# Requesting the first quarter of an output weight later, and longer warm-up matmuls between transposes

## The chip, the cores and the metric

The kernel runs on one core of a Trainium2 chip. The metric is device time in microseconds of one execution; the time before is the median of three runs. The profile is one execution taken by the hardware profiler, with a span of 687.3 us from its first to its last instruction.

## The reference

A causal depthwise convolution with seven taps (softmaxed weights, one set for each of eight groups of channels) feeds a two-layer network with a swish activation whose slope is learned:

```python
w = exp(weight - max(weight)); w = w / (sum(w) + 1e-9)      # 8 heads x 7 taps
y[b, s, h, g] = sum_k w[h, k] * x_pad[b, s + k, h, g]        # x: 8 x 4096 x 192, 6 zeros in front
h = y @ w_in                                                 # 32768 x 192 times 192 x 2048
g = h * sigmoid(beta * h)
out = g @ w_out                                              # 2048 x 192, result float32
```

## The kernel before, in words

The eight sequences are handled in pairs: a chunk is 512 tokens of two sequences, one on the lower 64 partitions and one on the upper 64, with the 192 channels as three groups of 64. There are 32 chunks. For each chunk the steady loop (from line 551) goes over 16 units `fc` of 128 columns of w_in: `hidden` (line 421) makes six matmuls of 512 columns into a PSUM tile `ph`, and ScalarE turns it into `g` with one Silu activation whose scale is beta. `output` (line 511) puts matmuls of the second layer between the units: a `Job` adds up 16 units times two blocks of 128 tokens in a PSUM slot `pa` or `pb`, then VectorE reduces it and it is stored. In the first chunk (s = 0) these begin with unit 6 (four pairs) and unit 7 (five pairs) in slot a; the fifth pair of unit 7 is the first to use unit 4 of w_out.

Since Silu with scale beta computes silu(beta * h), w_out is divided by beta once: `scale_w_out(i)` (line 314) multiplies quarter i of `w_out_raw` (units 4i to 4i + 3) by `beta_r` and rounds it to bf16. Quarters 0 and 1 are scaled on GpSimd (lines 360 and 362), quarters 2 and 3 on VectorE inside the first chunk. GpSimd also requests the w_in casts (`load_w_in`, line 205: a DMA that converts to bf16, in two halves of 64 partitions). Units 0 and 1 of w_in come instead by a plain load (`w_in_raw`, line 169) and a ScalarE cast (line 346).

All plain loads are requested on SyncE (its queue is q1 in the profile; the casts are q0), in the order of the program. Line 270 makes GpSimd wait for the softmax weights before it requests the casts of units 2 to 11 (lines 271 to 273). Line 275 then writes one column of `w_out_raw` on GpSimd; the load of that part must wait for this write, so SyncE stops there until GpSimd has requested the casts. After it come the w_out quarters, the load of chunk 2, the last quarter of w_out and the load of chunk 3. GpSimd's own queue goes on with: scale quarter 0 (waits for its load), request the last quarter of w_in (units 12 to 15), scale quarter 1 (waits for its load). [...]

Chunk 0 takes a way of its own. Its tokens are cast to `x0b` on VectorE (line 264), transposed on TensorE block by block (`transposes`, line 227, for four blocks), copied to `xt0` by ScalarE and VectorE (line 305), and convolved by matmuls with diagonal matrices (`diag_tap`, line 288). `fill(n, cols)` (line 216) issues n matmuls of zeros, whose result is not used: they keep TensorE active while it has nothing else to do. Chunk 1's first channel group is convolved on TensorE too (`conv1`, line 394), its other two by VectorE taps (`tap`, line 323), which run in the first chunk.

Of the kernel before, what the change touches and what calls it, by code (L numbers as in the profile page):

```python
# [17 lines left out]
def kernel(  # L18
# [17 lines left out]
    nc = tc.nc  # L36
# [96 lines left out]
    NW = 4  # L133
    FW = F // NW
    NQ = NF // NW
# [6 lines left out]
    w_out_raw = setup.tile([128, NF, D], FP32)  # L142
# [3 lines left out]
    def load_w_out(i):  # L146
        fcs = slice(i * NQ, (i + 1) * NQ)
        nc.sync.dma_start(out=w_out_raw[:, fcs, :], in_=w_out_v[:, fcs, :])
# [7 lines left out]
    def load_x(dst, t0, i):  # L156
        t = t0 + i * 2 * BLK
        nc.sync.dma_start(
            out=dst[:, i].rearrange("q h b d -> q h (b d)"),
            in_=x_v[0, t : t + 2 * BLK, :, :].rearrange("(q b) h d -> q h (b d)", b=2),  # L160
        )
# [6 lines left out]
    for r in range(2):  # L168
        nc.sync.dma_start(out=w_in_raw[r * DG : (r + 1) * DG], in_=w_in_v[:, :, 0:F0])
    load_x(x1, TOK, 1)  # L170
    load_w_out(0)

    zeros = setup.tile([128, 128], BF16)
    nc.vector.memset(zeros, 0.0)
# [13 lines left out]
        fill=0.0,  # L188
# [8 lines left out]
        fill=0.0,  # L197
# [18 lines left out]
    def fill(n, cols=TOK):  # L216
        zc = zeros.unsqueeze(1).to_broadcast((128, cols // 128, 128))
        for _ in range(n):
            nc.tensor.matmul(pf[:, 0, 0:cols], zeros, zc, start=True, stop=True)  # L219
# [7 lines left out]
    def transposes(pt, xb, b):  # L227
        for c in range(NG):
            nc.tensor.transpose(  # L229
                pt[:, c, :], xb[:, b, c].rearrange("q h p -> q (h p)"), ident_b  # L230
            )

    def tokens(xt, b):
        t = HALO + (b // 2) * 2 * BLK
        return xt[:, :, t : t + 2 * BLK].rearrange("p c (q b) -> p c b q", b=2)[:, :, b % 2]
# [3 lines left out]
    pw = in_a()[:, 0, 0:K]  # L239
    nc.tensor.matmul(pw, sel.rearrange("i h p -> i (h p)"), w8, start=True, stop=True)  # L240
    fill(3)
    nmax = setup.tile([128, 1], FP32)
    total = setup.tile([128, 1], FP32)
    cw = consts.tile([128, K], FP32)
# [10 lines left out]
    def diags(k0, k1):  # L255
        nc.vector.tensor_tensor(
            diag[:, k0:k1],
            ident.unsqueeze(1).to_broadcast((128, k1 - k0, 128)),
            cw[:, k0:k1].unsqueeze(2).to_broadcast((128, k1 - k0, 128)),
            ALU.mult,  # L260
        )
# [10 lines left out]
    for i in range(1, NW - 1):  # L272
        load_w_in(i * FW, (i + 1) * FW)

    nc.gpsimd.memset(w_out_raw[:, NQ, 0:1], 0.0)
    for i in range(1, NW - 1):
        load_w_out(i)
    load(2)
    load_w_out(NW - 1)
# [22 lines left out]
    for b in range(NB):  # L302
        pt = pts[b % 3][:, b // 3, 0 : NG * BLK].rearrange("p (c q) -> p c q", c=NG)
        transposes(pt, x0b, b)
        (nc.vector.tensor_copy if b == 2 else nc.scalar.copy)(tokens(xt0, b), pt)  # L305
        if b % 2:
            fill(1, 384 if b > 1 else 128)
    diags(2, 4)
    diags(4, K)
    pb = pf[:, 1, 0:NF]  # L310
# [315 lines left out]
```

## Time and profile before

| what | value |
|---|---|
| median of three runs | 689.9 us (690.95, 689.9, 689.1) |
| span of the profiled run | 687.3 us |
| TensorE matmuls busy | 681.8 us, 99% |
| ScalarE busy | 578.0 us, 84% |
| VectorE busy | 523.3 us, 76% |
| GpSimd busy | 10.2 us, 1% |
| w_out loads | 4 of 384 KB, 11.2 us from request to landing |
| w_in casts | 6 of 192 KB (8.5 us) and 2 of 96 KB (7.5 us) |

A row of a timeline gives start, length, engine, line, operation, output and inputs, and in brackets the idle time of the engine before it with what ended it. PE is TensorE's matmul, PEld its weight load, DVE is VectorE, ACT ScalarE, POOL GpSimd, SP SyncE; a q after the name means its sequencer. A matmul's end is modelled, and consecutive ones overlap in their records, so their spacing is read from the starts. Line numbers are those of the kernel before.

### The profile page before, as it was taken

Reading aid. Unit: us, or ns where it says so; the run is one execution under the profiler, and the core shown is the slowest. Engines: PE = TensorE matmul, PEld = TensorE weight load, DVE = VectorE, ACT = ScalarE, POOL = GpSimd, SP = SyncE. Lnnn points to the kernel's source line nnn. Section 1 sums busy time; section 2 is a strip of 40 time slices with the busy share of each in tenths; the row PEclk is TensorE's granted clock in tenths of the full one; section 3 lists DMA queues with packets and bytes.
Section 4 is the critical chain, followed back from the end, with each engine's and each line's share of the span. In section 5 each row is a group of like instructions: output and inputs, shape, how many; then the busy total and the mean of one; then the engine's idle time right before and its main releaser. Section 6 shows DMA issues by size and latency. Waiting matters only on the chain.

```text
span 687.3 us, 24341 instructions
## 1 busy us (share of the span) xinstructions
PE 681.8 (99%) x11311; PEld 520.4 (76%) x11311; DVE 523.3 (76%) x466; ACT 578.0 (84%) x529; POOL 10.2 (1%) x21
## 2 busy tenths in 40 slices
PE   8999999999999999999999999999999999999998
PEld 4777777777777777777777777777777777777777
DVE  7889877779777788777797777887777977777712
ACT  7988888888888888888888888888888888888893
POOL 4100000000000000000000000000000000000000
PEclk9999999999999999999999999999999999999999
DMA  9734433244343344332344332344423443322111
GB/s 234 185 101 117 111 94 103 57 103 117 99 101 83 71 116 116 94 99 67 92 117 105 96 98 58 111 117 105 92 67 88 117 111 94 100 58 60 49 36 59
DMA packets 121861, 67.06 MB, mean 98 GB/s; under 512 B 53264, under 2 KB 121760, under 8 KB 121760
## 3 DMA queue, kind: packets, MB, share of 16 engines
q1 hardware_dynamic: 120048, 64.12, 35.4%
q0 software_dynamic: 1664, 1.38, 1.2%
q8 instruction: 88, 1.44, 0.9%
q14 instruction: 13, 0.11, 0.1%
q10 hardware_dynamic: 48, 0.01, 0.0%
HBM read 29.89 MB, written 25.17 MB: 80 GB/s over the span
## 4 chain that ended last, share of the span: by engine, by line
PE 99%; DVE 1%; ACT 0%; issue 0%
PE ph L429 48%; PE pa L465 25%; PE pb L465 24%; PE pb L290 1%; DVE xt L383 0%; PE ph L219 0%; PE ph L290 0%; DVE x0b L222 0%; PE pa L290 0%; PE pa L240 0%; ACT xt L305 0%; ACT cw L246 0%; PE pb L373 0%; PE pa L229 0%; PE pb L229 0%
## 5 line engine op out<-in xcount | busy, mean ns | idle before, releaser
L437 ACT ACTIVATE g<-ph,beta 128x1024 bf16<-128x1024 f32 x511 | 568.6, 1115 | 94.0 <-PE ph L429 89.7
L465 PEld LDWEIGHTS <-g 64*128 64x128 bf16 x8160 | 370.0, 94 | 103.0 <-issue 0.2
L429 PE MATMUL ph<-ct,w_in_s 64*128 64x512 bf16 x3066 | 423.3, 376 | 0.0
L328 DVE SCALAR_TENSOR_TENSOR ct<-xt,cw,ct 128x1536 bf16<-128x1536 bf16 (+2 forms) x189 | 337.2, 1784 | 2.5
L465 PE MATMUL pa<-w_out_s,g 64*128 64x192 bf16 x4112 | 244.0, 243 | 0.0
L465 PE MATMUL pb<-w_out_s,g 64*128 64x192 bf16 (+1 forms) x4048 | 230.0, 243 | 0.0
L429 PEld LDWEIGHTS <-w_in_s 64*128 64x128 bf16 x3072 | 159.3, 94 | 53.6 <-issue 0.7
L483 DVE TENSOR_REDUCE osb<-pa 128x384 f32<-128x768 f32 x64 | 61.3, 958 | 122.6 <-PE pa L465 121.7
L483 DVE TENSOR_REDUCE osb<-pb 128x384 f32<-128x768 f32 x63 | 60.3, 958 | 29.0 <-PE pb L465 29.0
L106 DVE CAST xb<-xf 128x768 bf16<-128x768 f32 x60 | 40.5, 677 | 0.0
L326 DVE TENSOR_SCALAR ct<-xt,cw 128x1536 bf16<-128x1536 bf16 (+1 forms) x31 | 30.8, 993 | 0.0
L481 ACT COPY osb<-pb 128x192 f32<-128x192 f32 x1 | 0.3, 319 | 7.2 <-PE pb L465 7.2
L207 POOL DMA_DIRECT2D w_in_s<-in_moe_w_in_dram x8 | 5.2, 656 | 0.0
L290 PE MATMUL pb<-xt,diag 64*128 64x512 f32 (+1 forms) x21 | 4.6, 435 | 0.3 <-DVE xt L383 0.3
L219 PE MATMUL ph<-zeros 128*128 128x512 bf16 (+2 forms) x9 | 3.7, 526 | 1.1 <-DVE warm L176 1.1
L121 DVE COPY xt<-xt 128x18 bf16<-128x18 bf16 x27 | 4.4, 162 | 0.0
L290 PEld LDWEIGHTS pb<-xt,diag 64*128 64x128 f32 (+1 forms) x21 | 2.8, 186 | 1.2 <-PE ph L429 0.8
L316 POOL TENSOR_TENSOR w_out_s<-w_out_raw,beta_r 128x768 bf16<-128x768 f32 x2 | 3.3, 1648 | 5.9 <-DMA w_out_raw<-in_moe_w_out_dram 5.9
L177 ACT ACT_TABLE_LOAD x1 | 1.3, 1283 | 1.8 <-PEq L610 1.8
L219 PEld LDWEIGHTS <-zeros 128*128 128x128 bf16 x9 | 0.9, 120 | 1.9 <-DVE warm L176 1.1
L229 PEld LDWEIGHTS <-x0b 128*128 128x128 bf16 x12 | 0.7, 97 | 1.7 <-DVE x0b L222 1.7
L316 DVE TENSOR_TENSOR w_out_s<-w_out_raw,beta_r 128x768 bf16<-128x768 f32 x2 | 1.9, 952 | 0.0
(59 smaller groups left out, 29.9 us busy)
## 6 DMA issues: line engine op xcount, KB each, us to landing
out_dram<-osb SPq DMA_DIRECT2D x127, 192.0 KB, 2.3
xf<-in_x_dram SPq DMA_DIRECT2D x60, 384.0 KB, 4.2
xt<-xb SPq DMA_TRANSPOSE x120, 2.9
x<-in_x_dram SPq DMA_DIRECT2D x4, 384.0 KB, 4.7
w_out_raw<-in_moe_w_out_dram SPq DMA_DIRECT2D x4, 384.0 KB, 11.2
w_in_s<-in_moe_w_in_dram POOLq DMA_DIRECT2D x6, 192.0 KB, 8.5
w_in_raw<-in_moe_w_in_dram SPq DMA_DIRECT2D x2, 192.0 KB, 6.8
w_in_s<-in_moe_w_in_dram POOLq DMA_DIRECT2D x2, 96.0 KB, 7.5
```

Source lines behind the costliest of these rows:

```text
L106: nc.vector.tensor_copy(xbs[ch][:, :, :, h, :], xfs[ch][:, h].rearrange("q b (p c) -> q b c p", c=NG),)
L121: nc.vector.tensor_copy(dst, last[:, :, HALO + TOK - PAD :])
L207: nc.gpsimd.dma_start(out=w_in_s[r * DG : (r + 1) * DG, :, c0:c1], in_=w_in_v[:, :, c0:c1])
L219: nc.tensor.matmul(pf[:, 0, 0:cols], zeros, zc, start=True, stop=True)
L290: nc.tensor.matmul(pv, diag[rows, k, :], xt[rows, o : o + TOK], start=(k == 0), stop=(k == k1 - 1),)
L316: (nc.vector if i > 1 else nc.gpsimd).tensor_tensor(w_out_s[:, fcs, :], w_out_raw[:, fcs, :], beta_r[:, fcs].unsqueeze(2).to_broadcast((12 ...
L326: nc.vector.tensor_scalar_mul(dst, src, scalar)
L328: nc.vector.scalar_tensor_tensor(out=dst, in0=src, scalar=scalar, in1=added, op0=ALU.mult, op1=ALU.add)
L429: nc.tensor.matmul(ph[:, h, :], w_in_s[rows, j, fc * 128 : (fc + 1) * 128], cts[s][rows, j, :], start=(j == 0), stop=(j == last),)
L437: nc.scalar.activation(gs[s][:, fc], ph, AF.Silu, scale=beta[:, fc : fc + 1])
L465: nc.tensor.matmul(self.po[:, r, b * D : (b + 1) * D], g[rows, fc, self.h, q * BLK : (q + 1) * BLK], w_out_s[rows, fc, :], start=(self.don ...
L483: nc.vector.tensor_reduce(dst, self.po[:, :, 0 : nb * D].rearrange("p r n -> p n r"), axis=mybir.AxisListType.X, op=ALU.add,)
```

## The change

The first quarter of w_out is no longer requested early, ahead of the w_in casts. All quarters now stand behind the one-column write on GpSimd, which is moved to quarter 0: the casts of units 2 to 11 get the DMA engines first. Beside it the zero matmuls around chunk 0's transposes are made longer by 128 columns each in three places (after the three fills that follow the softmax matmul, after block 1 and after block 3), so that TensorE's pauses there are shorter.

```diff
@@ -168,7 +168,6 @@
     for r in range(2):
         nc.sync.dma_start(out=w_in_raw[r * DG : (r + 1) * DG], in_=w_in_v[:, :, 0:F0])
     load_x(x1, TOK, 1)
-    load_w_out(0)
 
@@ -239,6 +238,7 @@
     nc.tensor.matmul(pw, sel.rearrange("i h p -> i (h p)"), w8, start=True, stop=True)
     fill(3)
+    fill(1, 128)
     nmax = setup.tile([128, 1], FP32)
@@ -272,8 +272,8 @@
     for i in range(1, NW - 1):
         load_w_in(i * FW, (i + 1) * FW)
 
-    nc.gpsimd.memset(w_out_raw[:, NQ, 0:1], 0.0)
-    for i in range(1, NW - 1):
+    nc.gpsimd.memset(w_out_raw[:, 0, 0:1], 0.0)
+    for i in range(NW - 1):
         load_w_out(i)
     load(2)
     load_w_out(NW - 1)
@@ -304,7 +304,7 @@
         (nc.vector.tensor_copy if b == 2 else nc.scalar.copy)(tokens(xt0, b), pt)
         if b % 2:
-            fill(1, 384 if b > 1 else 128)
+            fill(1, 512 if b > 1 else 256)
     diags(2, 4)
```

## The prediction

> **What bounds the kernel now.** I read the busy shares first, then stages of the first 20 us, the chain, the timeline of GpSimd and VectorE, and the DMA queues. The busy shares and the busiest rows:
>
> ```profile
> PE 681.8 (99%) x11311; PEld 520.4 (76%) x11311; DVE 523.3 (76%) x466; ACT 578.0 (84%) x529; POOL 10.2 (1%) x21
> ```
>
> TensorE is busy 681.8 of 687.3 us. The stages say where the other 5.5 us lie (columns: stretch, its length, busy time and count of PE, PEld, DVE, ACT, POOL, granted clock, DMA share, GB/s):
>
> ```profile
> 0.00:4.34 4.34, 3.28 (x9) 1.21 (x9) 0.81 (x7) 2.10 (x5) 1.41 (x9) 1.00 0.51 151
> 4.34:7.14 2.80, 2.03 (x18) 0.92 (x16) 2.69 (x9) 2.55 (x6) 2.55 (x5) 1.00 0.99 281
> 7.14:11.30 4.16, 4.16 (x19) 3.15 (x20) 3.44 (x7) 2.64 (x5) 1.71 (x4) 1.00 1.14 274
> 14.50:14.83 0.33, 0.00 (x2) 0.04 (x2) 0.29 (x2) 0.33 (x2) 0.33 (x1) 1.00 1.19 239
> 14.83:20.00 5.17, 5.17 (x55) 3.57 (x57) 5.06 (x4) 4.92 (x6) 2.11 (x2) 1.00 1.15 276
> ```
>
> Idle are 1.06 us at the start, 0.77 us between 4.34 and 7.14, 0.33 us at 14.5, the rest in the tail after the last matmul. From 14.83 on TensorE never rests: whatever delays it there is added to the end, and nothing later gives it back. In the pauses before 7.14 it is not the bound; the chain there runs over other engines:
>
> ```profile
> 4.53 0.64 DVE x0b L222 x2
> 5.17 0.33 DVE diag L256
> 5.50 0.34 DVE x0b L222
> 5.83 0.05 issue
> 5.88 0.34 PE pa L229 x3
> 6.22 0.34 PE pb L229 x3
> 6.56 0.02 issue
> 6.58 0.51 ACT xt L305
> 7.10 0.04 issue
> 7.14 0.96 PE pa L290 x3
> ```
>
> The moved transfer feeds GpSimd, whose whole queue after 4.8 us is this (start, length, instruction, idle time before it):
>
> ```profile
> 4.83 3.91 POOL L207 DMA_DIRECT2D w_in_s<-in_moe_w_in_dram  x6
> 8.73 0.12 POOL L275 MEMSET w_out_raw<- 128x1 f32 x1
> 12.40 1.47 POOL L316 TENSOR_TENSOR w_out_s<-w_out_raw,beta_r 128x768 bf16<-128x768 f32 x1 [3.55 <-DMA w_out_raw<-in_moe_w_out_dram]
> 13.82 1.29 POOL L207 DMA_DIRECT2D w_in_s<-in_moe_w_in_dram  x2
> 17.47 1.83 POOL L316 TENSOR_TENSOR w_out_s<-w_out_raw,beta_r 128x768 bf16<-128x768 f32 x1 [2.37 <-DMA w_out_raw<-in_moe_w_out_dram]
> ```
>
> So it waits for the first quarter of w_out until 12.40, scales it, requests the last quarter of w_in, then waits for the second quarter until 17.47.
>
> [...] (2) [...] while GpSimd scaled at 17.47 to 19.30, the VectorE tap begun at 18.01 took 2.37 us where its neighbours take 1.285, and GpSimd finished 1.32 us after the tap before had ended (17.98). (3) [...] In this trace full clock is recorded from 4.34 us, 3.28 us after the first matmul, and held: the favourable case.
>
> **The short matmuls.** They add 128 columns after the three fills, 128 after block 1 and 128 after block 3. A cold 512-column fill spaces 0.426 us from the next (1.461, 1.887, 2.314), so 128 columns are 0.107 us cold[...]. The first falls into the 0.23 us in which TensorE waits for x0b (4.66 to 4.90), the second into the 0.26 us before 5.88, the third with the 0.23 us transpose of beta into the 0.27 us before 7.14. VectorE's casts and ScalarE's copy hide all three: **cost 0**. Their gain is 0 in a run whose clock is full at 4.34. [...] the cold stretch could run into the 17 diagonal matmuls after 7.14, spaced 0.23 us warm and at most 0.43 cold: 8 of them are 1.6 us. The three times before spread over 1.85 us, so this may be in them; for the median I take -0.1 us, bounds 0 and -1.6.
>
> **The moved request: what it removes.** Only one wait on w_in is visible: unit 4's first pair of matmuls starts at 15.36 and 15.54, where other pairs start within 0.04 us; its cast (second half) landed at 15.49, the trace says. Earlier casts give back **0.15 us**. Units 8 to 11 landed at 18.65 for a use at 20.08, so nothing is won there.
>
> **What it adds: a later landing.** The request goes from 4.34 to 8.88, when the memset releases SyncE; each of the other requests behind it shifts by its issue time, 0.4 us. Bounds from the trace: 12.4 (now; also 8.88 plus the 3.5 us of the first x load) and 17.34 (what the second quarter took, which was requested at this very 8.88). Between them I work with rates. Now w_out's bytes move in 8.7 to 10, then the casts almost alone, then both:
>
> ```profile
> q0 software_dynamic: 546, 0.39, 127.9%
> q1 hardware_dynamic: 25, 0.02, 3.8%
> ```
>
> ```profile
> q0 software_dynamic: 490, 0.47, 78.8%
> q1 hardware_dynamic: 451, 0.35, 38.6%
> ```
>
> The first pair is 10.5 to 12.5, the second 12.5 to 16: casts alone 0.195 MB/us; shared 0.134 and 0.100; q1 alone runs at 0.32 (0.58 MB in 16.2 to 18). The six casts are 0.98 MB, a quarter of w_out 0.39. If the casts take over at 8.7 and q1 joins at 12.5 as it did, casts have moved 0.74 by then and need 1.8 us more; q1 moves 0.18 in these and the rest in 0.66 us: 15.0, with some 0.5 us to completion (an estimate: almost nothing of the quarter moved after 11.5, and GpSimd was released at 12.4) **15.5**. If q1 joins at 10.0 (1.1 us after the request; the first request, at 0.81, shows its first bytes in the slice from 1 to 2 us), it needs 3.9 us: 14.4. If the casts do not start sooner than now, 17.3. I take 15.5.
>
> **Who is queued behind it.** GpSimd in order: scaling 0, the two requests for w_in's last quarter (1.29 us), scaling 1. At 15.5 VectorE is in a tap (taps stand back to back: one at 15.37 for 1.285, the next at 16.69). By (2) GpSimd starts at 16.66, ends at 17.98; first use of this quarter is at 18.68, in time. The requests take it to 19.3; scaling 1 meets the tap of 19.1 to 20.37 and ends at **21.7** instead of 19.30. Unit 7's last pair needs it at 19.98 (the tenth of the pa matmuls that start at 19.65): TensorE stands **1.7 us**. [...] The w_in requests come 4.2 us later, at 18.0 and 18.65; they took 7.5 and 8.4 us to land, 7.2 at best, so the second half lands at 25.9 to 27.1. Unit 12 uses it at 24.32, shifted to 26.0: 0 to 1.1 us more, which I take at 0 as the two overlap. VectorE loses nothing in sum: one collision with a tap before, one after, the other lying beside the PSUM evacuation of 20.3.
>
> **Sum:** 689.9 + 1.7 - 0.15 - 0.1 = 691.3.
>
> **The rivals.** A, the transfer is hidden anyway: w_out lands by about 13.5, scaling 0 runs beside copies out of PSUM, the second quarter's landing still decides scaling 1. For it: total bytes ahead of the second quarter are the same. Against: q1's gap of 10.5 to 12.5. 689.9 - 0.15 - 0.1 = 689.6. B, the landing is 17.3: GpSimd starts at 17.98, first use waits 0.6 us, requests at 19.3 and 19.95, scaling 1 done at 22.1 (2.1 us late), w_in's second half at 27.2 to 28.4 for 24.32: 2.8 to 4.0 us, say 693.2. For it: that is what the second quarter did from the same request time. C, the clock: the pauses now cost cold stretches in most runs and the fills end them: 688.4. Against: the profiled run (689.15 us) is warm at 4.34 already, and only 0.75 us under the median.
>
> **How the numbers follow.** Forecast 0.40 (spread 0.8 to 2.0 us over before), A 0.30, B 0.22, C 0.08. The bound of 0.3% is 2.07 us: slower are B and a tenth of the forecast's spread and a little more, 0.29; faster is half of C, 0.04; same 0.67. The range from 689.0 to 693.2 leaves out most of C and the late half of B.
>
> **What would show it.** Right: scaling 0 on GpSimd at 15 to 17.5 with its idle time ended by the w_out DMA, a TensorE pause of 1 to 2 us before the pa matmuls of unit 7, scaling 1 ending after 21. Step by step: x1b, taps and diagonal matmuls at the same times; unit 4's two halves within 0.04 us. A scaling that still starts before 13.5 makes A right; a pause at unit 12 for w_in makes B right; matmuls at 0.43 us spacing after 7.14 in the old trace only, or a median under 688.5, make C right. I would be wrong above all if the arbitration between the queues is not what the old order of bytes suggests.

## The result

The changed kernel takes **692.3 us** (median of six runs, 691.89 to 692.89) against 689.96 us before (six runs, 689.1 to 691.62): 2.3 us more, ratio 1.0031 with a 95% interval of 1.0018 to 1.0044. The forecast was 691.3, in a range that ends at 693.2. The direction, the place and the range were right. The loss was put too low (1.4 us forecast, 2.3 measured), and the two parts of the change do not add up as the forecast's sum supposed (experiments 1 and 2).

The profiled execution after the change spans 691.1 us. Its 3.8 us over the profile before are more than the medians' 2.3, because it is the longest of its six runs and the one before was among the shortest of its own; of what the runs before vary by, more below.

TensorE's busy time, first line of the page, rose by 1.4 us (683.2 for 681.8), so most of the 3.8 us is idle time:

```profile
PE 683.2 (99%) x11312; PEld 521.1 (75%) x11312; DVE 523.4 (76%) x466; ACT 578.0 (84%) x529; POOL 10.5 (2%) x21
```

It lies after 14.83 us, where TensorE never rested before. Stages, columns as before:

```profile
14.83:20.00 5.17, 4.79 (x44) 2.82 (x46) 5.06 (x4) 4.92 (x5) 2.89 (x3) 1.00 1.11 326
20.00:25.00 5.00, 3.75 (x57) 2.55 (x55) 4.95 (x6) 3.23 (x4) 1.91 (x2) 1.00 1.14 290
25.00:30.00 5.00, 3.75 (x56) 2.45 (x53) 3.49 (x7) 3.24 (x4) 0.00 (x0) 1.00 0.38 71
30.00:40.00 10.00, 10.00 (x166) 8.38 (x163) 5.83 (x7) 8.81 (x10) 0.00 (x0) 1.00 0.49 136
```

From 30 us on it is full again. TensorE's timeline names the stands, the stretches in which it waits. Two rows of the trace before, of the output matmuls of units 6 and 7 (the ninth matmul of the second row, which begins the fifth pair, starts at 19.98):

```profile
18.68 0.53 PE L465 MATMUL pa<-w_out_s,g 64*128 64x192 bf16 x8
19.65 0.61 PE L465 MATMUL pa<-w_out_s,g 64*128 64x192 bf16 x10
```

After the change (two stretches):

```profile
19.25 0.51 PE L465 MATMUL pa<-w_out_s,g 64*128 64x192 bf16 x8 [0.36 <-POOL w_out_s L316]
...
21.98 0.26 PE L465 MATMUL pa<-w_out_s,g 64*128 64x192 bf16 x2 [1.25 <-POOL w_out_s L316]
```

```profile
26.64 0.39 PE L429 MATMUL ph<-ct,w_in_s 64*128 64x512 bf16 x1 [0.16 <-DMA w_in_s<-in_moe_w_in_dram]
28.12 0.82 PE L429 MATMUL ph<-ct,w_in_s 64*128 64x512 bf16 x5 [1.10 <-DMA w_in_s<-in_moe_w_in_dram]
```

Scaling 0 is late for the first pa matmuls, scaling 1 for the fifth pair of unit 7, and the two halves of w_in's last cast are late for unit 12. Read by starts, the delay over the trace before grows from 0.57 us (19.25 for 18.68) to 2.0 (21.98 for 19.98) and to 3.6 and 3.8 (the two halves of unit 13, at 28.98 and 29.19 for 25.38 and 25.40). GpSimd's queue shows where all of it comes from:

```profile
17.11 2.09 POOL L316 TENSOR_TENSOR w_out_s<-w_out_raw,beta_r 128x768 bf16<-128x768 f32 x1 [8.24 <-DMA w_out_raw<-in_moe_w_out_dram]
19.15 1.29 POOL L206 DMA_DIRECT2D w_in_s<-in_moe_w_in_dram  x2
20.46 1.47 POOL L316 TENSOR_TENSOR w_out_s<-w_out_raw,beta_r 128x768 bf16<-128x768 f32 x1
```

GpSimd stands 8.24 us for w_out's first quarter, where it stood 3.55; the requests for w_in, which stand behind scaling 0 in its queue, go out at 19.15 instead of 13.82. The chain that ended last now has no work of TensorE between 3.5 and 28.1 us (its later part):

```profile
8.90 8.04 DMA w_out_raw<-in_moe_w_out_dram
...
17.11 2.09 POOL w_out_s L316
19.20 0.62 POOLq L621
19.82 8.26 DMA w_in_s<-in_moe_w_in_dram
...
28.12 0.69 PE ph L429 x5
```

Two transfers of 8 us, one requested only when the other has landed and been scaled.

### The profile page after: what moved, and what is told of

Its sections match the earlier page's. It is cut to its first block, busy times and chain, and to the rows that moved or that the text cites. A ratio compares the mean times of both kernels' runs of the same rounds, so it can differ in the third digit from the quotient of the medians.

```text
span 691.1 us, 24342 instructions
## 1 busy us (share of the span) xinstructions
PE 683.2 (99%) x11312; PEld 521.1 (75%) x11312; DVE 523.4 (76%) x466; ACT 578.0 (84%) x529; POOL 10.5 (2%) x21
## 4 chain that ended last, share of the span: by engine, by line
PE 96%; DMA 2%; POOL 1%; DVE 0%; ACT 0%; POOLq 0%; issue 0%
PE ph L429 47%; PE pa L465 24%; PE pb L465 24%; DMA w_in_s<-in_moe_w_in_dram 1%; DMA w_out_raw<-in_moe_w_out_dram 1%; POOL w_in_s L206 1%; POOL w_out_s L316 0%; PE ph L218 0%; POOLq L621 0%; PE pa L239 0%; ACT cw L246 0%; ACT osb L481 0%; POOL hold L270 0%; DVE cw L249 0%; DVE nmax L245 0%
```

## The experiments

The kernels of experiments 1 to 4 share one set of 30 runs of the kernel before (median 690.42 us), those of 5 to 8 another of 43 (690.24), those of 9 and 10 a third of 33 (689.62).

### 1 and 2: each part alone

```diff
 # 1, on the kernel before: the zero matmuls only
+    fill(1, 128)
-            fill(1, 384 if b > 1 else 128)
+            fill(1, 512 if b > 1 else 256)
 # 2, on the kernel before: the w_out request only
-    load_w_out(0)
-    nc.gpsimd.memset(w_out_raw[:, NQ, 0:1], 0.0)
-    for i in range(1, NW - 1):
+    nc.gpsimd.memset(w_out_raw[:, 0, 0:1], 0.0)
+    for i in range(NW - 1):
```

> The kernel before with only the longer zero matmuls. Theory 1 (the whole loss comes from the later w_out load, the zero matmuls cost nothing and save little): 689.3 to 690.0 us, ratio to before 0.999 to 1.000. Rival (the zero matmuls themselves delay the transposes): 690.5 us or more. Rival (the clock: they end a cold stretch that most runs of before have): 688.5 to 689.2 us with a narrower spread than before's 2.5 us.

> The kernel before with only the moved w_out request. Theory 1: 692.2 to 693.0 us, 2.3 to 3.1 above before; in its trace the scaling of quarter 0 on GpSimd starts near 17, TensorE stands three times: about 0.4 us before the first pa matmuls, 1.3 us before the fifth pair of unit 7, 1.3 us before unit 12. Rival (the zero matmuls are part of the loss): 691.5 us or less.

Measured: the zero matmuls alone 689.38 us (13 runs, ratio 0.9993, 0.9984 to 1.0001); the moved request alone 692.2 us (9 runs, ratio 1.003, 1.0019 to 1.0041), which are two groups, five runs at 691.7 to 692.2 and four at 693.1 to 693.2. So the loss is the request's: 1.8 us beside the 690.42 of the same set. Between kernel 1 and the changed kernel (692.3), which differ in it alone but were run in different sets, lie 2.9 us. The zero matmuls cost nothing. The interval does not show that they gain; the distribution points to it, with small counts: of the 30 runs before 13 were above 690.6 us, of kernel 1 one in 13. Once the request is moved no gain shows: 692.2 us without the longer zero matmuls, 692.3 with them.

The trace of kernel 2 fell into the upper group (693.13 us). Its TensorE after the transposes:

```profile
7.30 1.65 PE L289 MATMUL pa<-xt,diag 128*128 128x512 f32 x3
8.75 1.43 PE L289 MATMUL ph<-xt,diag 128*128 128x512 f32 x4
```

Three diagonal matmuls take 1.65 us where the profile before has 0.96; single ones start 0.427 us apart. In the clock's record full rate begins at 9.48 us here, at 4.34 in the profile before and at 5.55 in the changed kernel's. Yet the late clock does not make this run long. TensorE comes to the first pa matmuls 1.1 us late (19.82 for 18.68), and so does not wait for scaling 0 and stands only 0.45 us for scaling 1. Then it waits for w_in's second half, which lands at 28.29 (28.07 in the changed kernel), and unit 13's second half starts at 29.40, 0.2 us after the changed kernel's. The wait swallowed the cold stretch, and of the three stands expected there were two. Why kernel 2's runs fall into two groups stays open: no trace of the lower one was kept.

The start of full clock differs from trace to trace: in the 12 traces of this study it lies between 4.34 and 11.92 us. What decides on it is not shown.

### 3 and 5: what is queued behind the waiting scaling

```diff
 # 3, on the changed kernel: w_in's last quarter ahead of scaling 0
+    nc.gpsimd.tensor_copy(hold, beta_r[0:1, 0:1])
+    load_w_in((NW - 1) * FW, F)
     scale_w_out(0)
-    load_w_in((NW - 1) * FW, F)
     scale_w_out(1)
 # 5, on the changed kernel: w_in's last quarter behind scaling 1
     scale_w_out(0)
-    load_w_in((NW - 1) * FW, F)
     scale_w_out(1)
+    load_w_in((NW - 1) * FW, F)
```

> The changed kernel, with the requests for w_in's last quarter put ahead of the scaling of quarter 0 on GpSimd, behind a one-element copy that waits for beta_r (about 12.2 us). Theory 1a (what is queued behind the waiting scaling makes the larger part): the requests go out at 12.3 to 13.7, the stand at unit 12 (1.3 us) is gone, scaling 1 follows scaling 0 at once and ends near 20.6 instead of 21.9, so that the stand before it shrinks from 1.25 to some 0.3 us: 690.0 to 690.8 us. Rival 1b (the late landing alone makes the loss, the more so as the casts now also compete with w_out from 16 us on): w_out lands at 17.5 or later and the time stays at 691.7 or more.

> The changed kernel, with the scaling of quarter 1 put ahead of the requests for w_in's last quarter on GpSimd. Theory 3a (the last wait, for the second half of w_in's last quarter at unit 12, alone sets the loss and swallows the stands before it): the requests go out 1.5 us later than in the changed kernel, at 20.6 and 21.3, the second half lands near 29.5, and the time rises to 693.0 to 694.0 us although the stand before unit 7's fifth pair shrinks from 1.25 to below 0.4 us. Rival 3b (the stands for w_out make the loss): 691.0 to 691.6 us.

Measured: kernel 3 690.05 us (13 runs, 689.82 to 690.93), kernel 5 694.47 us (6 runs; ratio 1.0053, 1.0036 to 1.007). Both go the way of the queue: beside the changed kernel's 692.3 us, from another set, by 2.3 us down and 2.2 us up; counted from the kernel before in each one's own set, by 2.7 down and 1.9 up. In kernel 3, w_out lands hardly sooner (GpSimd is released at 16.37), yet most of the loss is gone. In kernel 5 the stand for scaling 1 has shrunk to some 0.3 us (the fifth pair of unit 7 starts at 20.33 for 20.00 undelayed, inside the first row of TensorE's), and still it is the slowest of all, a little above its expected range. Its GpSimd, and its TensorE:

```profile
16.23 4.05 POOL L316 TENSOR_TENSOR w_out_s<-w_out_raw,beta_r 128x768 bf16<-128x768 f32 x2 [7.37 <-DMA w_out_raw<-in_moe_w_out_dram]
```

```profile
19.67 0.91 PE L465 MATMUL pa<-w_out_s,g 64*128 64x192 bf16 x10
...
22.71 0.42 PE L465 MATMUL pb<-w_out_s,g 64*128 64x192 bf16 x6 [0.25 <-DVE ct L407]
27.41 0.39 PE L429 MATMUL ph<-ct,w_in_s 64*128 64x512 bf16 x1 [2.15 <-DMA w_in_s<-in_moe_w_in_dram]
28.42 0.82 PE L429 MATMUL ph<-ct,w_in_s 64*128 64x512 bf16 x5 [0.62 <-DMA w_in_s<-in_moe_w_in_dram]
```

The expected 29.5 for the second half was wrong: requested 1.07 us later than in the changed kernel (20.89 for 19.82), it landed only 0.3 us later, at 28.37. So the last wait is 0.3 us longer (28.42 for 28.12). The rest is clock, which no theory had: from 29.16 to 32.57 us the clock's record shows half rate (the mean granted clock is 0.92 from 25 to 30 us and 0.87 from 30 to 40; 1.00 in both in the changed kernel), by estimate half of these 3.41 us, 1.7 us, lost. The sum of 2.0 us is what lies between the two profiled runs (694.86 and 692.89). One of the six runs took 691.87 us; whether half clock was absent in it is not known, as it has no trace. Around the start of the half rate TensorE was less busy (from 25 to 30 us its matmuls filled 2.22 us, 3.75 in the changed kernel); that this is the cause is not shown. Without the clock kernel 5 stands about where the changed kernel does, though before unit 12 it was only 0.8 us late (unit 11 at 24.02 for 23.25), where that was 2.0: the wait for w_in's last quarter sets the loss, and swallows the stands for w_out before it. Kernel 3, which takes this wait away, confirms it from the other side.

When a load counts as complete varies by itself: five traces start alike (changed, 2, 3, 5 and 7), with the quarter's bytes moved at 15.1 to 15.2 us in each, and GpSimd is released at 17.11, 17.30, 16.37, 16.23 and 16.60. So the different releases of two of them say nothing about their edits.

### 4 and 6: when w_out is requested

```diff
 # 4, on the changed kernel: gate after four casts
     load_w_in(F0, FW)
-    for i in range(1, NW - 1):
-        load_w_in(i * FW, (i + 1) * FW)
+    load_w_in(FW, 2 * FW)
     nc.gpsimd.memset(w_out_raw[:, 0, 0:1], 0.0)
+    load_w_in(2 * FW, 3 * FW)
 # 6, on the changed kernel: gate after two casts
     load_w_in(F0, FW)
+    nc.gpsimd.memset(w_out_raw[:, 0, 0:1], 0.0)
     for i in range(1, NW - 1):
         load_w_in(i * FW, (i + 1) * FW)
-    nc.gpsimd.memset(w_out_raw[:, 0, 0:1], 0.0)
```

> The changed kernel, with the column write on GpSimd put ahead of the casts of units 8 to 11, so that w_out is requested at about 7.6 instead of 8.9 us. Theory 2a (a plain load requested while casts are on their way has its first bytes a fixed 3.6 us later): first w_out bytes at 11.2, quarter 0 lands near 15.7, 690.5 to 691.5 us. Theory 2b [...]: w_out quarter 0 flows directly behind x1 from about 8.7, lands near 12.5, and the time is that of before, 689.3 to 690.0 us. Theory 2c (only the amount of cast bytes ahead counts): first bytes near 11.8, landing near 16.3, 691.3 us or more.

> The changed kernel, with the column write on GpSimd put ahead of the casts of units 4 to 11, behind those of units 2 and 3 alone; w_out is requested at about 6.3 us. Theory 2a (first bytes a fixed 3.5 us after the request once casts are on their way): first w_out bytes at 9.8, mixed with casts; quarter 0 lands at 14.5 to 16, time 690.0 to 691.5. Theory 2b [...]: w_out behind x1 from 8.7, landing near 12.5 to 13.5, time 689.2 to 689.8, as with the early request and the zero matmuls.

Measured: kernel 4 692.63 us (5 runs), kernel 6 689.67 us (22 runs, ratio 0.9994, 0.9986 to 1.0001). In the packets' record w_out's first bytes flow at 11.3 us in kernel 4 and at 9.15 in kernel 6, 3.6 and 2.7 us after SyncE's request; behind the request of 8.9 us, before and after the change, it was 3.6 to 3.7. So the first bytes follow the request, as theory 2a has it, though the delay is not fixed: it was shorter with fewer casts ahead. That the casts are its cause is not shown: the kernel before requests quarter 0 at 4.34 us, ahead of every cast, and its first bytes flow at 8.40, behind the earlier loads of the same queue. And theory 2a's times failed in both kernels: kernel 4 lies in the range of 2c, whose landing stays near 17, kernel 6 in that of 2b. In kernel 4 the earlier bytes bought nothing. The two queues from 11 to 15 us there, and GpSimd:

```profile
q0 software_dynamic: 478, 0.45, 74.8%
q1 hardware_dynamic: 516, 0.39, 36.7%
```

```profile
17.09 2.27 POOL L315 TENSOR_TENSOR w_out_s<-w_out_raw,beta_r 128x768 bf16<-128x768 f32 x1 [8.29 <-DMA w_out_raw<-in_moe_w_out_dram]
```

By 15.0 q1 has moved 0.39 MB, as much as the quarter has, and still GpSimd is released two microseconds later. The changed kernel is alike: its packets reach that sum at about 15.15, its GpSimd starts at 17.11. Its queues from 15 to 16.5 us show what is left:

```profile
q1 hardware_dynamic: 601, 0.45, 103.0%
q0 software_dynamic: 23, 0.02, 7.8%
```

The casts still hold 7.8% of the engines' time, in a trickle. The traces keep 16 completion marks for each transfer. In kernel 2 the quarter has 15 of them by 16.00 us and the last at 17.12; in the changed kernel 13 by 15.98 and the last at 16.94; in kernel 5, released first, all 16 by 16.05. The last marks of w_in's last half straggle in the same way: 15 by 26.61 us and the last at 28.37 in kernel 5. That a few late marks of 16, at times a single one, end these waits is thus shown; what makes them late is not.

In kernel 6 w_out starts before the larger casts and is there in time:

```profile
13.14 1.47 POOL L316 TENSOR_TENSOR w_out_s<-w_out_raw,beta_r 128x768 bf16<-128x768 f32 x1 [4.34 <-DMA w_out_raw<-in_moe_w_out_dram]
```

### 7: the rest of kernel 3

```diff
 # on kernel 3
-    QUOTA_A = {6: 4, 7: 5}
+    QUOTA_A = {6: 4, 7: 4}
```

> The kernel with w_in's last quarter requested ahead of the scaling, and unit 7 of the first chunk given four pairs instead of five, so that quarter 1 is first used in unit 8, near 20.7 instead of 20.0 us. If the 0.4 us in which TensorE still stands between 20 and 25 us there is the wait for the scaling of quarter 1: 689.4 to 689.7 us, level with the zero matmuls alone (689.38). If it is the late end of the scaling of quarter 0 or another wait: 690.0 us, no change.

Measured: 690.05 us (14 runs), no change: what is left is set by another wait. Besides the 0.32 us before the fifth pair (20.32 for 20.00), which is gone in kernel 7, TensorE's timeline in kernel 3 has one stand between 16 and 30 us:

```profile
22.70 0.42 PE L466 MATMUL pb<-w_out_s,g 64*128 64x192 bf16 x6 [0.26 <-DVE ct L408]
```

Slot b waits for VectorE's evacuation of the diagonal convolution, which stands behind taps, and GpSimd's two scalings lie beside taps there (3.89 us for both, twice the 1.47 of each in kernel 6 are 2.94). The taps take longer too: the three beside the scalings 6.10 us in kernels 3 and 7, 5.01 in the kernel before, where one scaling lies beside them. In kernel 7 the stand for slot b is still there, 0.48 us long.

### 8, 9 and 10: the clock

```diff
 # 8, on the kernel before
-        if b % 2:
-            fill(1, 384 if b > 1 else 128)
 # 9 on kernel 6, 10 on kernel 1
-        if b % 2:
-            fill(1, 512 if b > 1 else 256)
+        if b != 2:
+            fill(1, (128, 384, 0, 512)[b])
```

> The kernel before without the two zero matmuls after blocks 1 and 3. Clock theory [...]: the runs fall apart into about 689.2 and 691.0 or more, more of them high than before (15 of 30 above 690.6 there), median 690.9 to 691.6. Rival (the pauses do not matter, the 1.0 us between before and the longer zero matmuls has another cause): 690.4 us and the same spread.

> The kernel whose column write on GpSimd stands behind the casts of units 2 and 3 alone (w_out requested at 6.3 us), with zero matmuls of 128, 384 and 512 columns after blocks 0, 1 and 3. If what is left of its spread (689.1 to 691.7) is the clock, [...] the runs draw together: median 689.2 to 689.4, hardly any above 690.6. If it is the DMA's timing: 689.6 us and the same spread.

> The kernel before with the longer zero matmuls, and with 128 and 384 columns after blocks 0 and 1. Clock theory: as with the shorter ones or a little better, 689.2 to 689.4 us; what stays above 689.9 are runs in which TensorE waits for the cast of units 4 to 7 (0.54 us in the profile of the longer zero matmuls alone). Rival (the added columns delay the transposes of the next block when the clock is low): 689.6 us or more.

Measured: without the two zero matmuls 690.71 us (14 runs, ratio 1.0002, 0.9991 to 1.0013), which lies between its two expectations, nine of 14 above 690.6 us against 18 of 43 before; kernel 9 689.71 us (13 runs, two above 690.6), kernel 10 689.37 us (21 runs, one above 690.6, against six of 33 before; ratio 0.9995, 0.9988 to 1.0001). No ratio is clear of 1, but the share of long runs falls with the columns in the pauses: 64% with none, 18 to 43% with those before (three sets), 8% and 5% with the longer ones on the same kernel. The sets ran on different chips and at different times, and kernel 8 differs from its own set by no more than chance allows; kernels 1 and 10 taken together (two of 34, against 37 of 106) by more. The longer ones do not end it: in kernel 7, which has them, five runs of 14 lie above 690.6 us and the trace (690.87) has full clock from 9.41 us. The trace of kernel 8 (691.37 us) has full clock from 11.92 us only:

```profile
8.76 3.19 PE L290 MATMUL ph<-xt,diag 128*128 128x512 f32 x7
```

Seven matmuls in 3.19 us, 1.79 in the profile before. Kernel 9's expected median of at most 689.4 us failed though its trace has full clock from 6.66 us; its median and spread (689.16 to 692.23) are nearer to its rival, the timing of the DMA. In its trace scaling 0 starts at 14.37 us, in kernel 6's at 13.14; whether that makes the spread is not shown. Kernel 10 came within its expected 689.2 to 689.4. No version is shorter than the kernel before by more than its interval; kernels 1, 6 and 10 come nearest.

## Why the prediction was right, and where it was not

**The bound.** TensorE never rests after 14.83 us, and a delay there is kept to the end: right for the last of the stands. A delay ahead of a later wait is swallowed by it, as kernels 2 and 5 show, so that stands do not simply add.

**The zero matmuls.** Cost 0 was right, kernel 1. The gain was taken as 0.1 us with 1.6 as the other bound; between the medians of before and kernel 1 lie 1.0 us, between those of before and kernel 10 0.25. The step that failed was to read one profiled run, warm at 4.34 us, as the usual one: it was the most favourable of the 12 traces. Rival C comes nearest in this part, though not in its time: no run of any kernel was below 689.08 us, and C's median was 688.4.

**The 0.15 us from earlier casts.** The two halves of unit 4 now start 0.03 us apart (15.41 and 15.44), as predicted, but nothing is gained: unit 5 starts at 16.71 for 16.68. It needs the PSUM tile of unit 3, and the activation that frees it begins at 15.54 for 15.51; ScalarE is the limit there. In some runs the wait is real, though: in the trace of kernel 1 the cast came later and TensorE stood 0.54 us for it.

**The landing.** Predicted 15.5, measured 17.0 (bounds 12.4 and 17.34). The bytes went as worked out from the order before, where q1 sent 480 packets and q0 18 from 8.7 to 10 us: casts take over by 8.7 to 9, q1 joins at 12.5, the quarter's sum is reached at 15.15 for 15.0. The mis-sized term is the half microsecond to completion, which was 1.8 (the last mark came at 16.94), and 0.9 to 2.0 in the other traces.

**The queue on GpSimd.** Right in its order and kind, but moved by that term. Scaling 0 ended at 19.2 and was late by 0.57 us, scaling 1 at 21.93 for the predicted 21.7, with 2.0 us of delay for the predicted 1.7. (What the prediction calls the tenth pa matmul at 19.98 is the ninth, first of the fifth pair.)

**Unit 12.** The second half of w_in's last quarter was put at 25.9 to 27.1 and its wait of 0 to 1.1 us at 0, "as the two overlap". It was requested 1.15 us later than forecast, took 8.26 us, inside the forecast's 7.2 to 8.4, landed at 28.07 and added 1.8 us to the 2.0. Here the forecast chose the wrong end: experiments 3 and 5 show that this wait, not scaling 1, decides. This is the costliest of the mis-sized terms. Rival B had this part nearly to the number (27.2 to 28.4, 2.8 to 4.0 us; 3.8 in the traces).

**The sum.** The forecast added the 1.7 us read from one trace of a run of 689.1 us to a median, 689.9, that contains runs with a late clock. The parts do not add in this way: before 690.42, zero matmuls alone 689.38, request alone 692.2, both 692.3 us. With the request moved, the wait for w_in can swallow what a late clock costs, as in kernel 2's trace, and the same move costs 1.8 us without the longer zero matmuls and 2.9 with them (from different sets). Two terms too small (1.7 for 3.8 in the trace), set on a median that counts the clock's loss again, gave a total 1.0 us off: that it came so near is in part luck.

## What to carry to other kernels

A load that is moved behind others is to be followed through the queue of the engine that waits for it: the costliest item may be a request for another transfer queued behind the wait, since its whole latency (8.26 us here) is then added once more, and the wait for it swallows the smaller ones before it. Put such requests ahead of the wait: that alone took the changed kernel from 692.3 to 690.05 us. And look at more than one execution before taking TensorE's warm-up from a profile: full clock began at 4.34 us in the one read here, at up to 11.92 in the others.

## What was not expected of the hardware

- A plain load requested while casts were on their way had its first bytes 2.7 to 3.7 us after the request, at 6.4, 7.7 or 8.9 us; the first load of the run needed 1.1. It need not be the casts: one requested at 4.34 us, ahead of them but behind other loads, needed 4.1.
- Half clock came back in mid-run, in kernel 5, from 29.16 to 32.57 us.
- The start of full clock ranged over 7.6 us in 12 traces (4.34 to 11.92), with nearly the same instructions in front of it.
- A transfer of 384 KB had 15 of its 16 completion marks by 16.00 us and the last at 17.12 (kernel 2): one straggler cost its waiter 1.1 us.
